# Output products two tiles behind the hidden products, in the expert stage of an attention and mixture-of-experts kernel

## The chip, the core and the metric

The kernel runs on one core of one Trainium2 chip. The metric is the device time of one execution in microseconds (us), as the median of several runs. The core's engines each work through a queue of their own, in the order in which the program was laid out: PE (TensorE, matrix products; its weight loads are listed apart as PEld), DVE (VectorE), ACT (ScalarE), POOL (GpSimd) and SP (SyncE, which here only starts transfers). Transfers (DMA) are also started from ACT and POOL. An instruction waits until the semaphores it needs are set, and everything behind it in the same queue waits with it.

## The reference, cut to what matters

Three stages follow one another. An attention between 512 tokens and 32 state rows, for 8 batches of 8 heads, gives 4352 rows of 512 numbers. A mixture of experts sends each row to one of 8 experts, 544 rows to each. A gated feed-forward layer closes.

```python
def _moe_ref(x, w_gate, w1, w2):
    ...
    for idx in order:                       # logits, from the largest down
        tok, e = (int(idx) // E, int(idx) % E)
        if assigned[tok] >= 0 or counts[e] >= cap:
            continue
        assigned[tok] = e
        counts[e] += 1
    ...
    for e in range(E):
        mask = assigned == e
        h = np.maximum(x[mask] @ w1[e], 0.0)
        out[mask] = h @ w2[e]

def _moe2_ref(x, w_gate, w_val, w_out):
    g = x @ w_gate
    silu = g * (1.0 / (1.0 + np.exp(-g)))
    return silu * (x @ w_val) @ w_out
```

w1 of an expert is 512 x 1024, w2 is 1024 x 512. The three matrices of the last layer arrive as 64-bit floats and are converted on the core.

## The kernel before

The attention takes the first 187 us of the profiled span, the experts run until about 691 us, and the last layer takes the rest. The change is in the experts.

**Tiles.** The 544 rows of an expert are worked in two halves, of 256 and 288 rows. For each half the 1024 hidden values come in 8 tiles of 128. So tile number u = 16 x expert + 8 x half + f, with f from 0 to 7, and there are 128 tiles. A matrix product of two 32-bit operands is done as three products of a high and a low part. `hidden` (L788) forms one tile of relu(x w1): 12 matmuls into the PSUM tile `h` (two buffers), then ACT writes the high part `hh` (L802) and DVE the low part `hl` (L803), each in a tile with two buffers. `expert_out` (L806) adds the tile's share of h w2 to the four PSUM tiles y0 to y3 (one buffer each): 8 matmuls that read `hh` (L813, L814) and 4 that read `hl` (L817). After f = 7 the four y tiles are copied to `ys`, y1 and y3 by ACT (L823), y0 and y2 by DVE (L825), and sent to memory. The next half's first output product writes the same four PSUM tiles, so it waits for these copies.

**Order.** The loop at the end of the stage (L995) issues, for each u, whatever the table `plan` holds for that u, then `hidden(u)`, then `expert_out(u-1)`. From there a scheduler lays out each engine's queue; `issue_after` ties an instruction behind a named one on its engine.

**What is woven in.** `plan` places between the tiles: the selection of the next expert's rows (`select`), a chain of short steps that go back and forth between DVE and PE (search steps L432 to L474, then the placement: sums over `C`, comparison `I` L421, `rh` L541, and 34 small matmuls L548 that read `rh`); the gathering of the selected rows and their transposition on PE through the PSUM tile `bt`, which has one buffer (`turn`, L777; ACT copies it to `xh` L782 and DVE to `xl` L783); the loading of the next expert's weights, 8 transfers of 512 KB, each followed by a cast on ACT (L725) and a subtraction on DVE (L726); and the conversion of the last layer's weights, in 36 pieces: `load64` starts a 512 KB transfer into `raw64` from ACT's queue (L167), and three tiles later `convert` scales it on ACT (`mag`, L175) and joins it on DVE (`f32v`, L177, L178, L180). The 36 transfers are planned at u = 10 + 3.2 n, so every fifth stands at u = 16k + 10, behind the hidden product of tile 16k + 9.

**Afterwards.** The last layer's operand tiles `yb` lie in a ring of 14 tiles of 4 KB per partition, split over two pools, `cy` and `cy2`, by `NY`.

Of the kernel before, what the change touches and what calls it, by code (L numbers as in the profile page):

```python
# [22 lines left out]
FR = mybir.dt.float32r  # L23
# [17 lines left out]
ROW = D + 1 + E  # L41
NT = 5
NW = 24
NY = (8, 6)
EARLY = 6
P_ = {'spin': 12, 'xl': 2, 'pc': (0, 9), 'ct': 12, 'cuts': (0, 34), 'lead': [0, 1, 10, 25, 44, 57, 73, 89], 'hook': ['p', 'p', 'p', 'p', 'p', 'x', 'p', 'p'], 'w': [8, 14, 8, 8, 8, 8, 8, 8], 'whook': 'h', 'g': [0, 3, 18, 36, 56, 70, 85, 103], 'gs': 0.34, 't': [0, 14, 29, 46, 61, 75, 91, 104], 'ts': 1, 'ghook': 'p', 'thook': None, 't0': (2, 4, 5), 'l0': 10, 'lp': 3.2, 'cd': 3, 'lhook': 'hh', 'chook': 'h', 'swap': [], 'y0': 16, 'f0': [10, 4, 3]}
PRE = 24
# [5 lines left out]
def f32(ap):  # L53
    return ap.bitcast(F32)
# [3 lines left out]
def moe_kernel(ctx: ExitStack, tc: tile.TileContext, x, state, moe_w_gate, moe_w1, moe_w2,  # L58
# [648 lines left out]
    bw = b_ctx.enter_context(tc.tile_pool(name="bw", bufs=2, reuse_waits="tile"))  # L707
# [81 lines left out]
    def hidden(i, hf, f):  # L789
        xh, xl = XT[i][hf]  # L790
        T = 256 + 32 * hf
        ph = bp.tile([128, 288], F32, name="h", bufs=2)[:, :T]
        fs = slice(128 * f, 128 * f + 128)
        terms = [(k, q) for k in range(4) for q in range(3)]
        if 16 * i + 8 * hf + f < P_["xl"]:
            terms.sort(key=lambda kq: kq[1])
        for n, (k, q) in enumerate(terms):
            hooks["p"] = nc.tensor.matmul(ph, W[i][0][k][q == 1][:, fs], (xl if q == 2 else xh)[:, k, :T],  # L798
                                          start=(n == 0), stop=(n == 11)).ins
        hh = bw.tile([128, 288], FR, name="hh")[:, :T]  # L800
        hl = bw.tile([128, 288], FR, name="hl")[:, :T]
        relu[16 * i + 8 * hf + f] = hooks["hh"] = nc.scalar.activation(hh, ph, AF.Relu).ins  # L802
        hooks["h"] = nc.vector.scalar_tensor_tensor(hl, ph, 0.0, f32(hh), op0=OP.max, op1=OP.subtract).ins  # L803
        return hh, hl

    def expert_out(i, hf, f, hh, hl):  # L806
        if f == 0:
            py[i, hf] = [bp.tile([128, 288], F32, name=f"y{d}")[:, :256 + 32 * hf] for d in range(4)]
        p = py[i, hf]
        wh, wl = W[i][1][f // 2]  # L810
        for d in range(4):
            ds_ = slice(128 * d, 128 * d + 128)
            nc.tensor.matmul(p[d], wh[:, f % 2, ds_], hh, start=(f == 0), stop=False)  # L813
            nc.tensor.matmul(p[d], wl[:, f % 2, ds_], hh, start=False, stop=False)  # L814
        for d in range(4):
            ds_ = slice(128 * d, 128 * d + 128)
            nc.tensor.matmul(p[d], wh[:, f % 2, ds_], hl, start=False, stop=(f == 7))  # L817
        if f == 7:
            T = 256 + 32 * hf
            ys = bw.tile([128, 4, 288], F32, name="ys", bufs=1)  # L820
            for d in range(4):
                if d % 2:
                    nc.scalar.copy(ys[:, d, :T], p[d])  # L823
                else:
                    nc.vector.tensor_copy(ys[:, d, :T], p[d])  # L825
            if hf == 0:
                nc.sync.dma_start(y_d[i][:, :, :256], ys[:, :, :256])
            else:
                nc.sync.dma_start(y_d[i][:, :, 256:], ys[:, :, :256])
                nc.sync.dma_start(yt_d[:, :, i, :], ys[:, :, 256:])  # L830
# [111 lines left out]
    def ring_tile():  # L942
        n = ring[0] % sum(NY)
        ring[0] += 1
        if n < NY[0]:
            return cy.tile([128, 2, 2, 256], FR, name="yb")
        return cy2.tile([128, 2, 2, 256], FR, name="yb")
# [44 lines left out]
        at(int(P_["l0"] + P_["lp"] * n), P_["lhook"], load64, n)  # L992
        at(int(P_["l0"] + P_["lp"] * n + P_["cd"]), P_["chook"], convert, n)

    pend = None  # L995
    for u in range(16 * E):
        i, hf, f = u // 16, u // 8 % 2, u % 8
        for hook, fn, args in plan.get(u, []):
            if hook:
                with tc.issue_after(hooks[hook]):  # L1000
                    fn(*args)
            else:
                fn(*args)
        if u in P_["swap"] and pend:
            expert_out(*pend)
            pend = None
        h = hidden(i, hf, f)
        if pend:
            expert_out(*pend)
        pend = (i, hf, f) + h  # L1010
    expert_out(*pend)
    sel_ctx.close()
    cy = ctx.enter_context(tc.tile_pool(name="cy", bufs=NY[0], side="right", reuse_waits="tile"))
    with tc.issue_after(relu[16 * E - P_["y0"]]):
# [12 lines left out]

    cy2 = ctx.enter_context(tc.tile_pool(name="cy2", bufs=NY[1], reuse_waits="tile"))
    cw = ctx.enter_context(tc.tile_pool(name="cw", bufs=1, reuse_waits="tile"))
# [281 lines left out]
```

## Time and profile before

| | us |
|---|---|
| median of 3 runs | 1485.01 |
| lowest and highest run | 1481.55, 1488.06 |
| profiled execution | 1485.12 |
| its span in the trace | 1483.5 |
| PE busy in the span | 1384.4 (93%) |
| DVE busy | 1126.4 (76%) |
| ACT busy | 571.0 (38%) |
| POOL busy | 468.2 (32%) |

The span is 1.6 us shorter than the profiled execution's own time. The profile gives, for each engine, how long it was busy, which instruction waited and what ended the wait ("releaser"), and the clock that TensorE was granted: 1.00 is its upper level of 2.4 GHz, 0.50 the lower of 1.2 GHz; a mean in between over a stretch says which part of it ran at which level. Of the chain of work that ended last, 71% is PE, 11% DVE, 8% DMA and 3% ACT.

### The profile page before, as it was taken

Reading aid. Unit: us, or ns where it says so; the run is one execution under the profiler, and the core shown is the slowest. Engines: PE = TensorE matmul, PEld = TensorE weight load, DVE = VectorE, ACT = ScalarE, POOL = GpSimd, SP = SyncE. Lnnn points to the kernel's source line nnn. Section 1 sums busy time; section 2 is a strip of 40 time slices with the busy share of each in tenths; the row PEclk is TensorE's granted clock in tenths of the full one; section 3 lists DMA queues with packets and bytes.
Section 4 is the critical chain, followed back from the end, with each engine's and each line's share of the span. In section 5 each row is a group of like instructions: output and inputs, shape, how many; then the busy total and the mean of one; then the engine's idle time right before and its main releaser. Section 6 shows DMA issues by size and latency. Waiting matters only on the chain.

```text
span 1483.5 us, 29094 instructions
## 1 busy us (share of the span) xinstructions
PE 1384.4 (93%) x11440; PEld 1335.4 (90%) x11441; DVE 1126.4 (76%) x2152; ACT 571.0 (38%) x1124; POOL 468.2 (32%) x398
## 2 busy tenths in 40 slices
PE   6998389998999999999999999999999999999997
PEld 5776278988988899999999999999999999999996
DVE  5898768876777765586888677976856797999982
ACT  5885124332332333343323232522323264444441
POOL 4775331100111001152553410012131002778872
PEclk9999579999999999999999999999999999999999
DMA  7542225545444356455665553635465378334431
GB/s 129 124 113 91 97 77 192 188 155 192 147 163 160 126 197 213 164 181 199 225 237 192 192 185 115 234 143 192 173 213 204 129 246 294 119 138 144 151 118 43
DMA packets 125417, 244.67 MB, mean 165 GB/s; under 512 B 48096, under 2 KB 57312, under 8 KB 118624
## 3 DMA queue, kind: packets, MB, share of 16 engines
q1 hardware_dynamic: 107696, 203.46, 40.6%
q10 hardware_dynamic: 11472, 19.43, 4.2%
q0 software_dynamic: 6112, 19.93, 3.9%
q8 instruction: 89, 1.46, 0.4%
q14 instruction: 48, 0.39, 0.1%
HBM read 157.84 MB, written 84.93 MB: 164 GB/s over the span
## 4 chain that ended last, share of the span: by engine, by line
PE 71%; DVE 11%; DMA 8%; issue 4%; ACT 3%; POOL 2%; SPq 0%; POOLq 0%; DVEq 0%; ACTq 0%
PE b L1044 44%; PE h L798 11%; PE y L817 4%; PE y L813 4%; PE y L814 3%; DMA raw<-in_moe_w_out_dram 2%; DMA raw<-v_d 1%; DMA raw<-in_moe_w_gate_dram 1%; DMA raw<-in_moe_w_val_dram 1%; DVE w L726 1%; PE bt L777 1%; DMA xc<-in_x_dram 1%; DVE xw L320 1%; DVE yb L842 1%; DMA raw<-in_moe_w_dram 1%
## 5 line engine op out<-in xcount | busy, mean ns | idle before, releaser
L1044 PE MATMUL b<-yb,w 128*128 128x256 f32 x4320 | 517.5, 282 | 6.9 <-DVE cs L1084 5.7
L1044 PEld LDWEIGHTS b<-yb,w 128*128 128x128 f32 x4320 | 515.0, 190 | 9.3 <-DVE cs L1084 7.2
L1044 PE MATMUL b<-w,yb 128*128 128x256 f32 x2160 | 257.2, 282 | 0.0
L1044 PEld LDWEIGHTS b<-w,yb 128*128 128x128 f32 x2160 | 257.0, 190 | 0.0
L798 PE MATMUL h<-xh,w 128*128 128x288 f32 (+1 forms) x1024 | 215.4, 303 | 0.7 <-issue 0.7
L798 PEld LDWEIGHTS h<-xh,w 128*128 128x128 f32 x1024 | 167.8, 197 | 1.7 <-issue 1.1
L768 POOL DMA_INDIRECT xg<-xm_d,idx x38 | 48.1, 1265 | 367.8 <-PE bt L777 163.4
L842 DVE TENSOR_TENSOR yb<-tt,yb 128x512 fp32r<-128x512 f32 x164 | 143.7, 893 | 14.4 <-ACT yb L841 14.4
L813 PE MATMUL y<-hh,w 128*128 128x288 f32 (+1 forms) x512 | 140.2, 300 | 12.6 <-DVE ys L825 4.8
L798 PE MATMUL h<-xl,w 128*128 128x288 f32 (+1 forms) x512 | 151.9, 299 | 0.0
L841 ACT CAST yb<-tt 128x512 fp32r<-128x512 f32 x164 | 101.2, 620 | 104.6 <-PE b L1044 87.8
L814 PE MATMUL y<-hh,w 128*128 128x288 f32 (+1 forms) x512 | 139.2, 298 | 0.0
L842 DVE TENSOR_TENSOR yb<-raw,yb 128x512 fp32r<-128x512 f32 x127 | 126.0, 1000 | 15.8 <-ACT yb L841 13.5
L864 POOL TENSOR_TENSOR tt<-raw 128x512 f32<-128x512 f32 (+1 forms) x33 | 42.0, 1277 | 286.9 <-DMA raw<-m_d 212.9
L802 ACT ACTIVATE hh<-h 128x288 fp32r<-128x288 f32 (+1 forms) x128 | 50.7, 397 | 199.2 <-PE h L798 177.5
L813 PEld LDWEIGHTS y<-hh,w 128*128 128x128 f32 x512 | 98.7, 194 | 14.9 <-ACT ys L823 6.3
L803 DVE SCALAR_TENSOR_TENSOR hl<-h,hh 128x288 fp32r<-128x288 f32 (+1 forms) x128 | 55.5, 435 | 69.6 <-ACT hh L802 63.7
L841 ACT CAST yb<-raw 128x512 fp32r<-128x512 f32 x127 | 78.1, 620 | 63.5 <-PE b L1044 50.2
L798 PEld LDWEIGHTS h<-xl,w 128*128 128x128 f32 x512 | 99.5, 196 | 0.2
L814 PEld LDWEIGHTS y<-hh,w 128*128 128x128 f32 x512 | 98.7, 194 | 0.3
L817 PE MATMUL y<-hl,w 128*128 128x288 f32 (+1 forms) x512 | 94.9, 300 | 2.2 <-DVE hl L803 2.2
L726 DVE TENSOR_TENSOR w<-raw,w 128x1024 fp32r<-128x1024 f32 x61 | 73.8, 1238 | 16.1 <-ACT w L725 15.4
(253 smaller groups left out, 2107.7 us busy)
## 6 DMA issues: line engine op xcount, KB each, us to landing
raw<-in_moe_w_dram SPq DMA_DIRECT2D x60, 512.0 KB
raw<-m_d SPq DMA_DIRECT2D x30, 1024.0 KB
m_d<-m SPq DMA_DIRECT2D x48, 512.0 KB
raw<-v_d SPq DMA_DIRECT2D x32, 512.0 KB
raw<-y_d SPq DMA_DIRECT2D x14, 1024.0 KB
v_d<-f32v SPq DMA_DIRECT2D x36, 256.0 KB
xm_d<-xm SPq DMA_DIRECT2D x8, 1024.0 KB
y_d<-ys SPq DMA_DIRECT2D x16, 512.0 KB
```

What stands on the lines that cost most here:

```text
L726: eng.tensor_tensor(lo, raw, f32(hi), OP.subtract)
L768: hooks["g"] = nc.gpsimd.indirect_dma_start(out=xg[:n], out_offset=None, in_=xm_d, in_offset=bass.IndirectOffsetOnAxis(ap=idx[i][:n, j:j + ...
L798: hooks["p"] = nc.tensor.matmul(ph, W[i][0][k][q == 1][:, fs], (xl if q == 2 else xh)[:, k, :T], start=(n == 0), stop=(n == 11)).ins
L802: relu[16 * i + 8 * hf + f] = hooks["hh"] = nc.scalar.activation(hh, ph, AF.Relu).ins
L803: hooks["h"] = nc.vector.scalar_tensor_tensor(hl, ph, 0.0, f32(hh), op0=OP.max, op1=OP.subtract).ins
L813: nc.tensor.matmul(p[d], wh[:, f % 2, ds_], hh, start=(f == 0), stop=False)
L814: nc.tensor.matmul(p[d], wl[:, f % 2, ds_], hh, start=False, stop=False)
L817: nc.tensor.matmul(p[d], wh[:, f % 2, ds_], hl, start=False, stop=(f == 7))
L841: nc.scalar.copy(hi, src)
L842: nc.vector.tensor_tensor(lo, src, f32(hi), OP.subtract)
L864: nc.gpsimd.tensor_tensor(S1, a21, a22, OP.add)
L1044: nc.tensor.matmul(p[:, q], a(x, q), b(y), skip_group_check=True, start=start and not (q or n or m), stop=stop and q == 1 and n == last an ...
```

## The change

The output products no longer follow one tile behind but two. `pend` becomes a list: after each `hidden` the oldest entries are worked off until two are left, or one where f = 0. So in a half the order is hidden(u), expert_out(u-2), except at its ends: behind hidden of f = 0 the last two output products of the half before come one after the other, and behind hidden of f = 1 there is none. `hh` and `hl` get a third buffer (2 x 288 x 4 = 2304 bytes more per partition), and the ring's split becomes 7 and 7 tiles. The branch on `swap`, an empty list, goes.

```diff
-NY = (8, 6)
+NY = (7, 7)
...
-        hh = bw.tile([128, 288], FR, name="hh")[:, :T]
-        hl = bw.tile([128, 288], FR, name="hl")[:, :T]
+        hh = bw.tile([128, 288], FR, name="hh", bufs=3)[:, :T]
+        hl = bw.tile([128, 288], FR, name="hl", bufs=3)[:, :T]
...
-    pend = None
+    pend = []
     for u in range(16 * E):
         i, hf, f = u // 16, u // 8 % 2, u % 8
...
-        if u in P_["swap"] and pend:
-            expert_out(*pend)
-            pend = None
-        h = hidden(i, hf, f)
-        if pend:
-            expert_out(*pend)
-        pend = (i, hf, f) + h
-    expert_out(*pend)
+        pend.append((i, hf, f) + hidden(i, hf, f))
+        while len(pend) > (1 if f == 0 else 2):
+            expert_out(*pend.pop(0))
+    for p in pend:
+        expert_out(*p)
```

The scheduler's order moves with it. First, PE at the border between tiles 111 and 112 (expert 6 to 7): from the last output matmul of the old half to the first of the new. `h_8677` is the hidden product of tile 113, `h_8694` below that of tile 114. Before:

```order
5228 L817 MATMUL y3_8412<-hl_8617,w_7611 128x288
5229 L798 MATMUL h_8677<-xh_8236,w_8286 128x256
...
5240 L798 MATMUL h_8677<-xl_8237,w_8304 128x256
5241 L813 MATMUL y0_8694<-hh_8654,w_8310 128x256
5242 L814 MATMUL y0_8694<-hh_8654,w_8311 128x256
```

And with the change:

```order
5236 L817 MATMUL y3_8438<-hl_8605,w_7599 128x288
5237 L798 MATMUL h_8677<-xh_8224,w_8274 128x256
...
5248 L798 MATMUL h_8677<-xl_8225,w_8292 128x256
5249 L798 MATMUL h_8694<-xh_8224,w_8274 128x256
...
5260 L798 MATMUL h_8694<-xl_8225,w_8292 128x256
5261 L813 MATMUL y0_8711<-hh_8642,w_8298 128x256
```

Two hidden products of 12 matmuls stand between the old half's last output matmul and the new half's first, where one stood. At the borders to tiles 32 and 64 the scheduler sets the first half of the new output product (y1 and y3), and the 34 placement matmuls behind it, between the two hidden products.

Second, ACT around the conversion that is loaded behind tile 105 (expert 6), where `hh_8405` is tile 105's. Before:

```order
523 L802 ACTIVATE hh_8405<-h_8392 128x288
524 L167 DMA raw64_8432<-in_moe2_w_gate_dram 128x2x512
525 L782 CAST xh_8238<-bt_8425 128x4x128
526 L175 ACTIVATE mag_8536<-raw64_8432 128x512
527 L802 ACTIVATE hh_8447<-h_8434 128x288
528 L725 CAST w_8310<-raw_8308 128x1024
529 L782 CAST xh_8238<-bt_8463 128x4x128
```

And with the change:

```order
523 L802 ACTIVATE hh_8405<-h_8392 128x288
524 L167 DMA raw64_8416<-in_moe2_w_gate_dram 128x2x512
525 L782 CAST xh_8226<-bt_8409 128x4x128
526 L802 ACTIVATE hh_8431<-h_8418 128x288
527 L175 ACTIVATE mag_8524<-raw64_8416 128x512
528 L782 CAST xh_8226<-bt_8451 128x4x128
529 L802 ACTIVATE hh_8471<-h_8458 128x288
```

The `hh` of tile 106 now stands ahead of `mag`, which waits for the transfer, instead of behind it; the copy of the next turned tile (`xh_8226<-bt_8451`) stands behind `mag`. Over all 36 pieces, 27 had one `hh` between the start of the transfer and `mag` and 9 had none; now 32 have one and 4 none.

Third, DVE at the placement of the last expert's rows, around tiles 89 and 90. Before:

```order
1098 L421 TENSOR_TENSOR I_7693<-IE_172,lo_7681 128x4352
1099 L726 TENSOR_TENSOR w_7594<-raw_7591,w_7593 128x1024
1100 L541 TENSOR_TENSOR rh_7690<-T6_7688,rq_1588 128x34x6 x2
1101 L803 SCALAR_TENSOR_TENSOR hl_7790<-h_7776,hh_7789 128x288
1102 L783 TENSOR_TENSOR xl_7449<-bt_7805,xh_7448 128x4x128
```

And with the change:

```order
1089 L421 TENSOR_TENSOR I_7693<-IE_172,lo_7681 128x4352
1090 L541 TENSOR_TENSOR rh_7690<-T6_7688,rq_1588 128x34x6 x2
1091 L803 SCALAR_TENSOR_TENSOR hl_7774<-h_7760,hh_7773 128x288
1092 L783 TENSOR_TENSOR xl_7437<-bt_7793,xh_7436 128x4x128
1093 L552 COPY dp_7730<-acc_7694 128x12
```

`rh` no longer stands behind the weight subtraction `w`. In the last layer the order of PE, ACT and DVE is the same as before.

## Rows read from the trace of the kernel before

**Rows 1.** Busy time by stretch: engines' us (instructions), granted clock, DMA share, GB/s.

```profile
187.00:691.00 504.00, 473.46 (x4120) 450.96 (x4120) 366.74 (x916) 171.77 (x328) 81.59 (x71) 0.96 0.49 165
```

**Rows 2.** Waits of PE, 187 to 700 us: total us, times, longest.

```profile
PE y L813 <- DVE ys L825: 4.8, 3, 2.0
PE y L813 <- ACT ys L823: 4.0, 2, 2.5
PE y L813 <- ACT hh L802: 3.9, 2, 2.4
PE y L817 <- DVE hl L803: 2.2, 3, 1.4
```

**Rows 3.** Timeline of PE where it idled: start, duration, instruction, idle time before.

```profile
342.12 0.39 PE L813 MATMUL y<-hh,w 128*128 128x256 f32 x1 [1.52 <-ACT hh L802]
368.21 1.05 PE L432 MATMUL acc<-G,I 128*128 128x8 bf16 x34 [2.53 <-DVE need L581]
422.15 0.40 PE L813 MATMUL y<-hh,w 128*128 128x288 f32 x1 [1.03 <-DVE ys L825]
430.76 0.16 PE L470 MATMUL acc<-fe,unit 32*128 32x8 bf16 x1 [2.24 <-DVE fe L468]
460.87 0.58 PE L813 MATMUL y<-hh,w 128*128 128x256 f32 x1 [2.55 <-ACT ys L823]
496.76 0.16 PE L470 MATMUL acc<-fe,unit 32*128 32x8 bf16 x1 [2.51 <-DVE fe L468]
527.25 0.39 PE L813 MATMUL y<-hh,w 128*128 128x256 f32 x1 [1.40 <-ACT ys L823]
564.25 1.01 PE L548 MATMUL acc<-rh,I 128*128 128x12 bf16 x34 [3.10 <-DVE rh L541]
620.65 0.47 PE L813 MATMUL y<-hh,w 128*128 128x288 f32 x1 [2.37 <-ACT hh L802]
643.43 0.36 PE L813 MATMUL y<-hh,w 128*128 128x256 f32 x1 [1.72 <-DVE ys L825]
668.93 0.38 PE L813 MATMUL y<-hh,w 128*128 128x288 f32 x1 [2.05 <-DVE ys L825]
```

**Rows 4.** Timeline of ACT and its DMA queue (ACTq): three conversion loads.

```profile
451.18 0.35 ACTq L167 DMA_DIRECT2D raw<-in_moe_w_out_dram  x1
459.87 0.66 ACT L175 ACTIVATE mag<-raw 128x512 f32<-128x512 f32 x1 [4.68 <-DMA raw<-in_moe_w_out_dram]
...
553.59 0.39 ACTq L167 DMA_DIRECT2D raw<-in_moe_w_gate_dram  x1
560.78 0.66 ACT L175 ACTIVATE mag<-raw 128x512 f32<-128x512 f32 x1 [3.60 <-DMA raw<-in_moe_w_gate_dram]
...
611.07 0.41 ACTq L167 DMA_DIRECT2D raw<-in_moe_w_gate_dram  x1
619.64 0.66 ACT L175 ACTIVATE mag<-raw 128x512 f32<-128x512 f32 x1 [5.94 <-DMA raw<-in_moe_w_gate_dram]
```

**Rows 5.** Stretches of 8 us behind three of the stalls; clock third from the end.

```profile
430.00:438.00 8.00, 7.24 (x68) 6.34 (x67) 5.25 (x15) 1.92 (x4) 0.00 (x0) 1.00 0.03 11
460.00:468.00 8.00, 7.13 (x65) 7.04 (x66) 3.12 (x16) 1.96 (x6) 2.55 (x3) 0.57 0.43 136
496.00:504.00 8.00, 7.24 (x52) 6.47 (x51) 5.25 (x13) 2.28 (x5) 0.95 (x1) 0.79 0.13 37
```

**Rows 6.** Chain of waits: one product of 12 matmuls, 256 and 288 wide.

```profile
281.00 1.43 PE h L798 x12
...
670.76 1.59 PE h L798 x12
```

**Rows 7.** Timeline of DVE, before the placement matmuls and before tile 120's product.

```profile
562.40 1.22 DVE L726 TENSOR_TENSOR w<-raw,w 128x1024 fp32r<-128x1024 f32 x1 [3.39 <-ACT w L725]
563.55 0.64 DVE L541 TENSOR_TENSOR rh<-T,rq 128x204 bf16<-128x204 bf16 x2
...
669.04 0.68 DVE L178 SCALAR_TENSOR_TENSOR f32v<-mag,f32v 128x512 int32<-128x512 int32 x1
```

## The prediction

> **What bounds the kernel now.** I read the busy time by stretch first. In the expert stretch PE works 473.46 of 504.00 us and DVE 366.74, at a mean granted clock of 0.96 [rows 1]. So PE sets the time there, and two things are to be had: about 30 us in which it idles, and the time at the lower clock. The change touches nothing that the attention or the last layer computes, so the sum is made over this stretch.
>
> Next come PE's waits, grouped by what ended them [rows 2]. The output products waited 8.8 us for the copies `ys` that free the four y tiles (4.8 for DVE, 4.0 for ACT), 3.9 us for `hh` and 2.2 us for `hl`: 14.9 us, half of the idle time. These are the waits that a longer lag can reach. The rest is mostly selection, small matmuls that wait for DVE.
>
> PE's timeline shows where the large ones lie [rows 3]: five waits for `ys` (1.03, 2.55, 1.40, 1.72, 2.05 us; all at the first output product of a new half), two for `hh` (1.52, 2.37), and four of the selection (2.53, 2.24, 2.51, 3.10).
>
> Then the queue that is late. ACT starts a conversion load and some instructions later stands at `mag` until it lands: 8.7 us after the start in the first pair of rows, 7.2 and 8.6 in the others, with ACT idle for 3.60 to 5.94 us [rows 4]. All that is queued behind `mag` is late with it: `hh`, the `ys` copies, weight casts, and through them DVE. The loads behind tile 16k+9 meet the next expert's weights, and there the four selection waits and the `hh` wait of 2.37 us lie.
>
> Last, the clock. After the wait of 2.55 us the next 8 us ran at 0.57, after 2.51 us at 0.79; after 2.24 us at 1.00 [rows 5]. What that costs is 8 x (1 - clock): 3.4 and 1.7 us. The stretch behind 368.21 read 0.57 as well, and those behind 527.25, 564.25 and 620.65 read 0.79; behind 342.12, 422.15, 643.43 and 668.93 the clock stayed up. So these six falls cost 2 x 3.4 + 4 x 1.7 = 13.6 us. Which stall brings a fall is not a matter of its length alone, since 1.40 us did and 2.05 us did not.
>
> **The change part by part.** A product of 12 matmuls takes 1.43 us at 256 columns and 1.59 us at 288 [rows 6]; I call that a phase. No matmul is added or removed; the number of phases is the same, and only their order differs.
>
> *At a border of halves* the new half's first output product waits for the old half's copies. Between them stood one hidden product, now two [the order of PE in the section on the change]: 1.43 to 1.59 us more cover. Counted from work tied to the old half's last tile, an output product comes in as well, so 2.9 to 3.2 us. By place:
> - 422.15 (tile 56): 1.03 goes to 0.
> - 460.87 (tile 64): `ys` stands behind `mag` in both orders, and here the first half of the output product stays ahead of the second hidden product, so only one phase comes in: 2.55 - 1.6 = 0.95.
> - 527.25 (tile 80): 1.40 goes, but the 34 placement matmuls now stand inside the hidden product of tile 81 and wait for `rh`. The trace of before has no such wait here; it lies between 0 and the 3.10 of 564.25. I take 0.9, what 564.25 comes to below.
> - 643.43 (tile 112): 1.72 against 3.0 more: 0. Three more ACT casts now precede `ys`, so up to 1.72 may stay.
> - 668.93 (tile 120): 2.05 - 3.0, but two conversion steps of 0.68 [rows 7] now precede the copies on DVE: 0.4.
> Together 8.75 to 2.25: 6.5 us gained. If DVE's backlog is as late as its worst row, the gain falls to 4.
>
> *Waits for `hh`.* At 342.12 `mag` stood ahead of the next `hh`; now it stands behind it, and the output product comes two phases later: 1.52 goes. The placement matmuls come two tiles earlier there, and I take 0.8 for them (0 to 3.10, as above). Gain 0.7. At 620.65 the order of ACT changes likewise, but one `xh` copy now stands behind `mag`. PE's fifth transposition needs the single `bt` tile, hence that copy and the subtraction on DVE. From tile 105's `hh` PE has two transpositions, two hidden and two output products to do, about 7.3 us; `mag` ends at 619.64 + 0.66 - 611.07 = 9.2, and two steps near 0.68 [rows 7] follow: 10.5. A wait of 3.2 in place of 2.37: 0.8 lost, bounded by 1.6 either way (one phase).
>
> *Behind tile 16k+9* the lag works backwards. No output product follows f = 1, so from there to any later hidden product, and to the selection steps tied to it, PE has one phase less to do, while the load takes as long as before. Four selection waits lie there:
> - 368.21: 1.6 less cover, but `need` now goes ahead of the weight subtraction (1.22 [rows 7]): 0.4 more.
> - 430.76 and 496.76: the step that meets `mag`'s delay is a later one; I take 0.3 and 0.9 more (at 496.76 a turned tile's subtraction goes ahead of it). Bounds are 0 and 1.6 each.
> - 564.25: `rh` stood behind a weight subtraction (562.40 to 563.62) that had waited 3.39 us for its cast; DVE had been free since 559.01 [rows 7]. Now `rh` goes first and could end at 559.01 + 0.64 = 559.7. PE arrived at 564.25 - 3.10 = 561.15, now 2.4 earlier by the order (the placement stands in tile 91, not in tile 90's output product): 558.8. Wait 0.9, gain 2.2; not below 0, so the gain is 3.10 at most.
> Net 0.6 gained.
>
> *Early tiles.* Of the 2.2 us for `hl` [rows 2], 0.6 and a placement wait beside it go and a wait for tile 9's `hl` comes; I take 0.4 gained. The wait of 1.4 in the first tiles stays, since the next search step waits for the same DVE chain.
>
> *Buffers and pools.* The third `hh` and `hl` buffers cost no instruction. The ring's eighth tile moves to the pool that opens after the experts; its first write comes about 15 us later, with seven tiles ready. I take 0; the wait that the last layer already has at 715 us could move by as much as 3 us either way.
>
> Direct: 6.5 + 0.7 - 0.8 + 0.6 + 0.4 = 7.4 us. Clock: with 460.87, 527.25 and 564.25 below 1.1 us, I take their falls as gone (3.4 + 1.7 + 1.7), since 1.03 brought none; a longer wait near 430.76 may bring one (1.7). Net 5.1. The bounds are 0 (new falls elsewhere) and 10. Sum: 12.5 us off the profiled 1485.12, about **1473 us**; the median of the runs, 1485.01, is the same number.
>
> The Trainium skill has a rule against this: in "TensorE: Matmul & The Clock Gate", section "HAM oscillation", a kernel whose matmuls waited for transfers was helped by the order of its loop, and PSUM double-buffering on top gave no further gain. By it the time would stay near 1485, the first rival's side; the waits at 368.21 to 496.76 agree with it, and the five for `ys`, of which three lie behind no load, do not.
>
> **The rivals.**
> *The waits only move (no change).* Half of the stalls come from loads that land when they land. If the five places behind tile 16k+9 (368.21, 430.76, 496.76, 564.25, 620.65) each lose a whole phase, 5 x 1.6 = 8 in place of the net 0.2 lost above, and the clock falls as often as now, 6.5 + 0.7 + 0.4 - 8 = -0.4: 1485.5; with the clock's gain at 460.87 and 527.25 kept, 1480. For it: those loads take 7.2 to 8.6 us [rows 4] against four or five phases of PE's work. Against: 564.25 and 368.21 lose a subtraction ahead of them.
>
> *The border costs more than it gives (slower).* Behind f = 1, hidden(8k+3) needs the `h` tile that hidden(8k+1) wrote, so `hl` of 8k+1 has 3.2 us where it had 4.2, and the single `bt` tile is asked for a phase earlier. If at the six loads behind 16k+9 from 295 us on PE loses 1.6 us and the clock falls to 0.57 each time (6 x 3.4 = 20.4 in place of the 8.5 now at 368, 496, 564 and 620): +9.6 + 11.9 - 7.6 (`ys`, `hh`, early) - 5.1 (clock at 460, 527) = +8.8: 1494. It decides once each of the six costs over 3.4 us more than now. For it: the falls follow just such stalls. Against: `hh` of 8k+2 now stands ahead of `mag`.
>
> *All of it goes.* If the selection finds DVE free as well, 14.9 of `ys`, `hh` and `hl` and 10 of clock: 1460. Against: that chain alternates PE and DVE whatever the lag.
>
> That the change doesn't do what it says is excluded by PE's order, but for tiles 32 and 64.
>
> **How the numbers follow.** Forecast (1467 to 1478) 0.54; waits only move (1479 to 1489) 0.28; slower 0.10; all goes 0.08. The range takes the forecast and most of the first rival: 1465 to 1488. A measurement of this kernel can tell about 0.5%, or 7.4 us, from no change. Faster by more: 0.50 of the forecast and the 0.08, 0.57 together; slower by more: 0.10; same: 0.33.
>
> **What would show it.** Right: PE's waits for `ys` fall from 8.8 us below 3 and those for `hh` and `hl` below 2; no fall of the clock behind tiles 64 and 80; the wait for `rh` near tile 91 below 1.5 us; a wait of PE's transposition for `xl` near tile 108. Wrong: waits of L798 for `hl` or `hh` (the `h` tile not free) of more than 3 us in total, falls of the clock at places that had none, or idle time of PE in the experts that is not below 26 us.

## The result, and the profile after

The change makes the kernel faster: 1469.4 us against 1481.4 (medians of 8 runs each), ratio 0.9919, 95% interval 0.9895 to 0.9943. In a later session (6 runs, 11 of before) it was 1473.3 against 1483.2, ratio 0.9936 (0.9911 to 0.9961). The forecast was 1473, which is 12.5 us less than the profiled 1485.1; the medians lie 12.0 apart.

The gain lies where the sum was made. The first view is busy time by stretch, from the first hidden product of tile 0 to the end of tile 127's output product; the columns are the stretch, its length, PE's busy time, its matmuls, the mean granted clock, the DMA share and GB/s. Before:

```profile
188.30:691.48 503.18, 473.31 (x4121) 0.96 0.49 165
```

After, in its first profile:

```profile
188.44:679.06 490.62, 467.71 (x4121) 0.96 0.51 169
```

And in a second profile of the same kernel:

```profile
185.46:675.42 489.96, 467.26 (x4120) 0.96 0.50 169
```

The stretch is 12.6 and 13.2 us shorter. The matmuls are the same, so length minus busy is idle time, and a change of busy time is put down to the clock. Idle time fell from 29.9 to 22.9 and 22.7 us, busy time by 5.6 and 6.1. The forecast was 7.4 of waits and 5.1 of clock. In the first profile the whole span fell by only 9.2, from 1483.5 to 1474.3, because there the last layer took 795.2 us for 792.0. In the second profile it took 791.5. So the order alone does not bring that loss, which stays an open point below; the first profiled execution was also the slowest of its eight, at 1475.9.

PE's waits in the experts after the change (engine, line and tile, what ended the wait: total us, times, longest), for the groups of [rows 2]:

```profile
PE bt L777 <- DMA xg<-xm_d,idx: 3.9, 1, 3.9
PE bt L777 <- DVE xl L783: 3.2, 2, 1.9
PE acc L432 <- DVE G L406: 3.1, 1, 3.1
PE h L798 <- DVE hl L803: 2.5, 3, 1.4
PE acc L466 <- DVE ev L463: 2.5, 3, 2.0
PE y L813 <- DVE ys L825: 2.0, 3, 0.9
...
PE y L813 <- ACT ys L823: 0.6, 2, 0.3
```

The waits for `ys` went from 8.8 to 2.6 us (1.4 of it at the five places of [rows 3], the rest at two borders that had none), those of the output products for `hh` from 3.9 to none. Three of the large groups are new: the transposition that waits for gathered rows, the one that waits for `xl`, and the search step that waits for `G`. The first and the last lie together in time, as PE's timeline shows (start, duration, instruction; in brackets the idle time before it and what ended it). These rows answer to [rows 3]:

```profile
247.71 0.66 PE L777 MATMUL bt<-ident,xg 128*128 128x128 f32 x4 [3.87 <-DMA xg<-xm_d,idx]
...
251.52 1.17 PE L432 MATMUL acc<-G,I 128*128 128x8 bf16 x34 [3.14 <-DVE G L406]
...
371.52 1.03 PE L432 MATMUL acc<-G,I 128*128 128x8 bf16 x34 [1.99 <-DVE need L581]
...
494.51 0.24 PE L466 MATMUL acc<-ev,SL 128*32 128x8 f16 x4 [1.98 <-DVE ev L463]
...
555.87 0.66 PE L777 MATMUL bt<-ident,xg 128*128 128x128 f32 x4 [1.25 <-DVE xl L783]
...
610.08 0.43 PE L777 MATMUL bt<-ident,xg 32*128 32x32 f32 x4 [1.93 <-DVE xl L783]
...
658.14 0.37 PE L813 MATMUL y<-hh,w 128*128 128x288 f32 x1 [0.88 <-DVE ys L825]
```

At the first two rows PE stands for 7 us of 8. Nothing like it was there before: in the same stretch of before PE was busy all the time, though the DMA was as full.

```profile
238.00:246.00 8.00, 7.89 (x60) 1.00 1.01 369
246.00:254.00 8.00, 8.00 (x96) 1.00 0.39 116
```

After:

```profile
238.00:246.00 8.00, 5.06 (x34) 1.00 0.97 320
246.00:254.00 8.00, 3.12 (x44) 0.68 0.37 131
```

The gather starts on POOL at 239.61 and its rows are there at 247.7. Before, it started at 237.73, and the transposition stood two products later in PE's queue, so nothing was seen of it.

Last, the clock in stretches of 8 us, as in [rows 5]:

```profile
250.00:258.00 8.00, 6.46 (x72) 0.64 0.22 43
372.00:380.00 8.00, 8.00 (x65) 0.58 0.24 68
434.00:442.00 8.00, 7.78 (x67) 1.00 0.31 99
460.00:468.00 8.00, 7.71 (x91) 1.00 0.74 236
494.00:502.00 8.00, 7.49 (x54) 0.79 0.04 12
527.00:535.00 8.00, 8.00 (x70) 1.00 0.68 213
555.00:563.00 8.00, 7.13 (x55) 1.00 0.53 171
610.00:618.00 8.00, 7.92 (x49) 0.79 0.52 163
```

The falls behind tiles 64, 80 and 91 are gone, none came near 430, those at 372, 494 and 610 stayed, and one is new at 250.

### The profile page after: what moved, and what is told of

It reads as the page before. It is cut to its first block, busy times and chain, and to the rows that moved or that the text cites. A ratio compares the mean times of both kernels' runs of the same rounds, so it can differ in the third digit from the quotient of the medians.

```text
span 1474.3 us, 29106 instructions
## 1 busy us (share of the span) xinstructions
PE 1381.2 (94%) x11441; PEld 1334.0 (90%) x11441; DVE 1121.4 (76%) x2152; ACT 570.2 (39%) x1124; POOL 465.5 (32%) x398
## 4 chain that ended last, share of the span: by engine, by line
PE 72%; DVE 10%; DMA 8%; issue 5%; ACT 3%; POOL 1%; SPq 0%; POOLq 0%; DVEq 0%; ACTq 0%
PE b L1041 48%; PE h L798 10%; PE y L813 3%; PE y L817 3%; PE y L814 3%; DMA raw<-in_moe_w_val_dram 1%; DMA raw<-in_moe_w_gate_dram 1%; DMA raw<-in_moe_w_out_dram 1%; PE bt L777 1%; DMA raw<-v_d 1%; DMA xg<-xm_d,idx 1%; DVE xw L320 1%; DMA raw<-in_moe_w_dram 1%; DVE xTl L232 1%; DVE I L421 1%
## 5 line engine op out<-in xcount | busy, mean ns | idle before, releaser
L813 PE MATMUL y<-hh,w 128*128 128x288 f32 (+1 forms) x512 | 137.6, 295 | 2.6 <-DVE ys L825 2.0
L814 PE MATMUL y<-hh,w 128*128 128x288 f32 (+1 forms) x512 | 136.7, 293 | 0.0
L817 PE MATMUL y<-hl,w 128*128 128x288 f32 (+1 forms) x512 | 91.0, 295 | 0.0
L1048 ACT ACTIVATE m<-b 128x256 f32<-128x256 f32 x60 | 22.9, 383 | 165.0 <-PE b L1041 147.7
```

The source lines that it names most:

```text
L1048: nc.scalar.activation(m, g, AF.Sigmoid)
```

## The experiments

The theory held that the lag covers the copies `ys` and ACT's standing at `mag`, and that the new wait near 248 us limits the gain. The rivals: one of the parts (border, lag inside a half, buffers) does all of it, or the lag only covers the loads. In the table, the stretch and PE's idle time in it are from one profile each (first hidden product to last output product, as above).

| kernel | stretch | idle | median | ratio to before, 95% |
|---|---|---|---|---|
| before | 503.2 | 29.9 | 1481.4 | |
| changed | 490.6 | 22.9 | 1469.4 | 0.9919 (0.9895 to 0.9943) |
| changed, again | 490.0 | 22.7 | 1473.3 | 0.9936 (0.9911 to 0.9961) |
| border only | 497.9 | 27.6 | 1477.9 | 0.9981 (0.9960 to 1.0002) |
| inside a half only | 491.1 | 25.2 | 1474.9 | 0.9980 (0.9960 to 1.0001) |
| buffers only | 503.7 | 29.1 | 1477.4 | 0.9993 (0.9969 to 1.0017) |
| two buffers | 486.0 | 21.9 | 1471.2 | 0.9948 (0.9926 to 0.9970) |
| before, convert later | 490.7 | 22.5 | 1471.8 | 0.9932 (0.9905 to 0.9958) |
| changed, turn later | 491.5 | 22.5 | 1472.0 | 0.9913 (0.9883 to 0.9942) |
| changed, convert later | 488.4 | 22.5 | 1465.2 | 0.9896 (0.9870 to 0.9922) |
| both (turn and convert later) | 480.2 | 19.5 | 1462.7 | 0.9871 (0.9845 to 0.9897) |
| both, selection later | 480.2 | 16.2 | 1458.0 | 0.9859 (0.9829 to 0.9888) |
| changed, lag of three | 487.3 | 22.2 | 1470.0 | 0.9948 (0.9927 to 0.9969) |

Medians of before differ between sessions: 1480.0 beside the four kernels from "border only" to "two buffers", 1483.2 beside "changed, again", "before, convert later", "changed, turn later" and "both", and 1478.9 beside the last three that were made ("changed, convert later", "both, selection later", the lag of three). So kernels of different sessions are compared by their ratios.

The columns "stretch" and "idle" are of one execution each, and two things in them are no effect of an edit. The profiled executions of the changed kernel (the first), "border only", "changed, convert later" and "both, selection later" were the slowest of their kernels, 6.5 to 9.3 us above the median. And the clock of the first 30 us of the stretch differed: it read 0.73 or 0.74 in eight profiles, those of before and both of the changed kernel among them, but 0.81 in "border only" and "both, selection later", 0.84 in "inside a half only", and 0.89 in "two buffers" and in "both". The hidden product of tile 8 starts 38.5 us into the stretch in the changed kernel and in "changed, convert later", 34.1 us into it in "both", though these three have the same order up to there. So 4.4 us of what "both" seems to gain in its stretch belong to that execution.

**Border only.**

```diff
-        while len(pend) > (1 if f == 0 else 2):
+        while len(pend) > (2 if f == 1 else 1):
```

> Only the border of two halves is changed: two hidden products stand between the old half's last output product and the new half's first, and inside a half the output product follows one tile behind, as before. Theory (the gain lies at the border): PE's waits for ys fall from 8.8 us to under 3, the falls of the clock behind tiles 64 and 80 go, the waits of the output products for hh (3.9 us) stay, and PE has no wait for the gathered rows near 248 us; 1468 to 1474 us, ratio to before 0.991 to 0.996. Rival (the gain is the lag inside a half): 1478 to 1483, ratio over 0.997.

Measured: 1477.9, ratio 0.9981. `ys` fell to 1.8 us, as the theory said, and there was no wait for gathered rows. But the 1.8 us lie at tile 80, where the fall of the clock stayed (0.79 in 520 to 528), and the stretch gained only 5.3. PE's waits show where the rest went:

```profile
PE acc L466 <- DVE ev L463: 4.0, 2, 2.1
...
PE bt L777 <- DVE xl L783: 3.6, 1, 3.6
...
PE y L813 <- ACT ys L823: 1.8, 1, 1.8
PE y L813 <- ACT hh L802: 1.7, 1, 1.7
```

The selection's waits for `ev` were 1.0 before and are 4.0, while those for `fe` went from 5.9 to 1.5; in all the selection waits as long as before (15.7 us for 14.9). The wait for `xl` is new. Taking the `ys` waits away brings PE sooner to the next late thing. The theory that the gain lies at the border falls.

**Lag inside a half only.**

```diff
-        while len(pend) > (1 if f == 0 else 2):
+        while len(pend) > (1 if f < 2 else 2):
```

> The counterpart: the output products follow two tiles behind inside a half, but at a border only one hidden product stands between the halves, as before. Theory (border): PE's waits for ys stay at 6 us or more, those for hh go, the wait for the gathered rows near 248 us is there as in the changed kernel; 1476 to 1484 us, ratio 0.996 to 1.002. Rival (lag inside a half): 1468 to 1474, ratio under 0.995, with the hh waits gone.

Measured: 1474.9, ratio 0.9980, a time between the two ranges. By the ratio neither part alone can be told from no change, though the median of this one lies 5.1 us below that of before in the session and the border's 2.1. In its profile the stretch is 12.1 us shorter. Some 3 of that were gained before tile 8, which starts 3.1 us sooner than in the changed kernel; the rest is still more than the border's 5.3. The expectation for `ys` failed:

```profile
PE y L813 <- DVE ys L825: 2.5, 1, 2.5
...
PE y L813 <- ACT yb L841: 1.7, 1, 1.7
```

Only 4.2 us are left of 8.8, though one hidden product stands at the border as before. (The 1.7 are the wait at the border to tile 112; the view puts them down to `yb`, which stands behind the copies `ys` in ACT's queue.) So either phase alone covers over half of the `ys` waits, which is why the two parts do not add there. A likely reason, argued and not shown: with a second output product behind the new half's first hidden product, `hh` and `hl` of the new tile are done before the old half's y tiles are complete, and no longer hold up the copies.

**Buffers only.** The order of before, with the third `hh` and `hl` and the ring's split:

```diff
-NY = (8, 6)
+NY = (7, 7)
...
+        hh = bw.tile([128, 288], FR, name="hh", bufs=3)[:, :T]
+        hl = bw.tile([128, 288], FR, name="hl", bufs=3)[:, :T]
```

> The order of before with only the third hh and hl buffers and the ring's tiles divided 7 and 7. Theory: nothing, 1478 to 1484, ratio 0.998 to 1.002, the waits for ys and hh as before. Rival (the buffers or the pools carry the gain): 1467 to 1474, ratio under 0.995.

Measured: 1477.4, ratio 0.9993, the waits as before (`ys` 9.4, `hh` 4.0). The buffers alone do nothing that can be told from no change, as forecast.

**Two buffers.** The new order with those lines as before.

> The new order with two hh and hl buffers and the ring divided 8 and 6, as before. Theory (the order carries the gain; a relu that waits for the output product before it is one phase late and has a phase of room): 1468 to 1477, ratio 0.991 to 0.997. Rival (the third buffer is needed, since relu and the hl subtraction hold up all that is queued behind them on ACT and DVE): 1481 or more, with waits of the hidden products for hl over 5 us.

Measured: 1471.2, ratio 0.9948. The hidden products' waits for `hl` were 3.0 us, not over 5. The order carries the gain; that the third buffer adds to it is not shown, since the intervals overlap.

**The changed kernel again.**

> The changed kernel once more, on the chip of the three runs beside it and with a second profile. Theory (its first profile, at 1475.9 us, stands above its own median by 6.5 us, and the loss lies in attention and the last layer): 1467 to 1473 us, ratio to before 0.990 to 0.996; again a wait of 2 to 5 us of PE's transposition for the gathered rows near 248 us, one of about 3 us for the next selection step, and a clock below 0.7 behind them. Rival (that wait was an accident of one execution): no wait over 1 us there.

Measured: 1473.3, ratio 0.9936, just above the expected 1467 to 1473. The waits near 245 us were there again, 3.14 for the rows and 3.14 for `G`. They belong to the order, not to one execution.

**Transposition later.**

```diff
-            at(P_["t"][k] + int(j * P_["ts"]), P_["thook"], turn, k, j)
+            at(P_["t"][k] + int(j * P_["ts"]), "p" if k == 1 and j == 0 else None, turn, k, j)
```

> The changed kernel, but the first transposition of expert 1 is tied to the hidden product of tile 13, so that it stands behind the output product of tile 11 in PE's queue instead of in front of the selection for expert 2. Theory (that transposition waits for its gather and holds up the selection behind it, 3.9 + 3.1 us and a fall of the clock of 3 us): the waits at 247 to 255 us fall from 7 to under 2 us, the clock stays over 0.9 there, and 1459 to 1466 us, ratio to before 0.985 to 0.991, 0.994 to 0.997 of the changed kernel. Rival (the selection only waits for something else, or the later transpositions delay the first tiles of expert 1): within 2 us of the changed kernel.

Measured: 1472.0, beside 1473.3 for the changed kernel on the same chip: the rival. The wait for rows is gone, but PE's timeline shows what took its place:

```profile
241.63 0.18 PE L580 MATMUL acc<-crb,onesb 128*128 128x8 bf16 x1 [1.29 <-DVE crb L578]
...
244.95 1.17 PE L432 MATMUL acc<-G,I 128*128 128x8 bf16 x34 [3.14 <-DVE G L406]
```

The 3.14 us stayed to the hundredth, and so did the fall of the clock (0.57 in 242 to 250). In this kernel's order, as in the changed one's, the 34 matmuls of L432 stand right behind the one of L580, with no product of the experts between. DVE's rows of the changed kernel show what they wait for:

```profile
248.44 0.17 DVE L581 TENSOR_SCALAR need<-acc 128x8 f32<-128x8 f32 x1 [3.02 <-PE acc L580]
...
251.03 0.43 DVE L406 TENSOR_TENSOR G<-w,am 128x272 bf16<-128x272 f32 x1
```

DVE stands at `need` until L580 is done, and `G` is six instructions behind it, 3.0 us. `G` itself takes nothing from `need` or from L580; it is late because its steps stand behind `need` in DVE's queue. That wait of 3.14 is in all seven profiles whose queue has L580 and L432 side by side here, and in none of the six where a product stands between (before, border only, buffers only, two buffers, before with the conversion later, and the selection later). My theory blamed the transposition for this wait; it is the selection's order.

**Conversion later, on the order of before.** Each of the 36 weight conversions follows its load by four tiles, not three:

```diff
-P_ = {... 'cd': 3, ...}
+P_ = {... 'cd': 4, ...}
```

> The order of before, but each weight conversion follows its load by four tiles instead of three, so that ACT does not stand at mag until the load lands. Theory (half of what the lag gains is cover for ACT standing at mag, the rest is the border itself): the waits for hh (3.9 us) and the ys wait of tile 64 go, ys keeps 4 to 6 us at the other borders, the clock falls at 460, 497, 564 or 620 become fewer; 1471 to 1478 us, ratio 0.994 to 0.999. Rival (all of the gain is cover for ACT at mag): ys under 2 us as well, 1464 to 1471, ratio under 0.993.

Measured: 1471.8, ratio 0.9932, a little more gain than the theory expected: as much as the change's, by another way. ACT's waits at `mag` for the load, in the experts, before:

```profile
ACT mag L175 <- DMA raw<-in_moe_w_val_dram: 21.6, 7, 8.0
ACT mag L175 <- DMA raw<-in_moe_w_out_dram: 18.4, 9, 4.7
ACT mag L175 <- DMA raw<-in_moe_w_gate_dram: 14.4, 6, 5.9
...
ACT mag L175 <- DVE f32v L178: 4.2, 5, 1.7
```

With the conversion later:

```profile
ACT mag L175 <- DVE f32v L178: 33.8, 15, 4.9
...
ACT mag L175 <- DMA raw<-in_moe_w_val_dram: 14.3, 3, 6.9
ACT mag L175 <- DMA raw<-in_moe_w_gate_dram: 13.6, 3, 6.0
...
ACT mag L175 <- DMA raw<-in_moe_w_out_dram: 2.1, 1, 2.1
```

The waits for the load went from 54.4 us in 22 to 30.0 in 7. But `mag` has one buffer, so it now waits for the DVE step L178 that reads the piece before: whatever ended the wait, ACT stood at `mag` for 66.9 us before and for 71.0 with the conversion later. So the edit does not shorten ACT's standing; it changes what ACT stands for, and where. Which of this brings the gain is not shown. And of the 30.0 us, 25.5 are the five loads behind tile 16k+9, the worst ones, which took 28.4 before. In the changed kernel the waits for the load sum to 57.6 in 23 (48.4 in 20 in its second profile): the lag takes little or nothing off them, it lets PE get past them. The `ys` waits kept 4.3 us, as the theory said; that of tile 64 is gone, and the clock fell three times where it had fallen six times. The `hh` waits did not go (3.1).

**Conversion later, on the changed kernel.**

> The changed kernel with only the weight conversions four tiles behind their loads. Theory (the lag and the later conversion add, since the lag gives cover at the ends of halves and the later conversion takes ACT's standing at mag away): 1462 to 1468 us, ratio to before 0.986 to 0.992, and the wait of PE's transposition for xl near 610 us (1.9 to 2.4) under 1. Rival (the combined kernel's gain came from both edits together, and the lag covers the loads already): 1469 to 1474 us.

Measured: 1465.2, ratio 0.9896, as the theory said; but the wait for `xl` near 609 us was 2.8, where under 1 was expected. On ACT one sees why: there a single `hh` stands between the start of the load and `mag`, as in the changed kernel, and `mag` waits for the load as before, with the copy `xh` behind it.

```profile
599.09 0.39 ACTq L167 DMA_DIRECT2D raw<-in_moe_w_gate_dram  x1
...
601.01 0.41 ACT L802 ACTIVATE hh<-h 128x288 fp32r<-128x288 f32 x1 [0.90 <-PE h L798]
607.08 0.66 ACT L175 ACTIVATE mag<-raw 128x512 f32<-128x512 f32 x1 [5.65 <-DMA raw<-in_moe_w_gate_dram]
607.64 0.57 ACT L782 CAST xh<-bt 128x512 fp32r<-128x512 f32 x1
```

**Both edits together.** The two diffs above, on the changed kernel.

> The changed kernel with both edits: the first transposition of expert 1 later, and each weight conversion four tiles behind its load. Theory (the two losses that are left, near 250 us and behind tile 16k+9, are separate and add): 1454 to 1463 us, ratio to before 0.981 to 0.989, with PE's idle time in the experts under 15 us and at most two falls of the clock behind 230 us there. Rival (with two tiles of lag the loads are covered already, so the later conversion adds nothing): as the run with the later transposition alone, within 2 us.

Measured: 1462.7, ratio 0.9871, whose interval lies below that of the changed kernel in the same session. Idle time was 19.5, not under 15, the wait for `G` was still there, and the clock fell three times (near 241, 364 and 600), not at most twice.

**Selection later.** The combined kernel, and:

```diff
-P_ = {... 'hook': ['p', 'p', 'p', 'p', ...], ...}
+P_ = {... 'hook': ['p', 'p', 'h', 'p', ...], ...}
```

> The combined kernel, and the selection for expert 2 is tied to the subtraction hl of tile 10 instead of its hidden product, so that PE has a hidden product and part of an output product between the first small matmul of its new search step and the 34 that wait for DVE. Theory (it is this order, not the transposition, that brings the waits of 2.4 and 3.1 us near 240 us and the clock of 0.57 behind them): both waits under 1 us, no fall of the clock there, 1454 to 1460 us, ratio to before 0.981 to 0.986. Rival (the selection of expert 2 then ends later, and the gathers for expert 2 or a later step wait instead): 1461 to 1466 us.

Measured: 1458.0, ratio 0.9859. The 3.14 us are gone, as they must be if the order of the selection brings them. But two smaller waits stand there now, not under 1 us as expected:

```profile
244.42 0.18 PE L580 MATMUL acc<-crb,onesb 128*128 128x8 bf16 x1 [1.75 <-DVE crb L578]
...
245.93 0.85 PE L798 MATMUL h<-xh,w 128*128 128x288 f32 x2 [1.33 <-DVE hl L803]
```

The clock fell behind them as it did in the combined kernel (0.57 in 245 to 253; there 0.57 in 241 to 249), where no fall was expected. Idle time fell by 3.3 us, and yet the stretch is as long as the combined kernel's. The difference lies in the first 30 us, where both have the same order. Combined, and with the selection later:

```profile
187.11:217.11 30.00, 27.07 (x247) 0.89 0.21 73
...
189.23:219.23 30.00, 25.12 (x211) 0.81 0.21 74
```

The profiled execution was the slowest of this kernel, 9.3 us above its median. The two ratios overlap, so the times do not show that this edit adds to the combined kernel. It has the lowest ratio of the study; its interval lies below the changed kernel's.

**A lag of three.** Four `hh` and `hl` buffers, and:

```diff
-        while len(pend) > (1 if f == 0 else 2):
+        while len(pend) > min(3, f + 1):
```

> The changed kernel with output products three tiles behind, and four hh and hl buffers. Theory (two tiles already cover ys and hh, of which under 3 us of waits are left, and what remains is selection, which the lag does not reach): 1467 to 1476 us, ratio to before 0.990 to 0.998, ys waits under 3 us as with two. Rival (more of the same cover still helps): under 1466 us, ratio under 0.990.

Measured: 1470.0, ratio 0.9948, as the theory said. No wait for `ys` is left, and another came:

```profile
PE h L798 <- DVE hl L803: 6.2, 3, 4.7
```

The longest of them, 4.74 at 625.47, is at tile 115, where on DVE steps of the last layer's operands (`yb`) stand ahead of `hl`.

## Why the prediction was right, point by point

The time was right, 1473 for 1469.4 and 1473.3, and so were the two sums: 7.0 and 7.2 us of idle time for 7.4 forecast, 5.6 and 6.1 of busy time for 5.1 of clock. The mechanism, more cover for the waits on `ys` and `hh`, was right too. But inside the first sum errors cancelled, and that it came so near is in part luck: all steps but the early tiles were to give 7.0 us and gave about 14, and the early tiles, which were to give 0.4, lost about 7 (13 and 6 in the second profile).

- *Border.* 8.75 to 2.25 was forecast; 1.4 at these places (2.6 with two other borders) and 1.3 were measured. That both phases count, as the step had it, is shown by the two halves of the change, which leave 1.8 and 4.2.
- *`hh` at 342.12.* Gone. The 0.8 set against it for `rh` did not come.
- *620.65.* The mechanism was right: PE's transposition waits for `xl` behind `mag`. The size was 1.93 and 2.37, not 3.2, because that load took 7.2 us, not the 8.6 of [rows 4].
- *Behind tile 16k+9.* The four selection waits, 10.4 us in [rows 3], were forecast to give 0.6 and came to 5.5 (1.99, 0.23, 1.98, 1.25) and 6.2 in the second profile. So this step was mis-sized by about 4, to the good. The loads there were quicker than in the kernel before [rows 4]; at tile 41, `mag` begins 7.3 us after the load's start:

```profile
362.68 0.35 ACTq L167 DMA_DIRECT2D raw<-in_moe_w_out_dram  x1
...
369.95 0.66 ACT L175 ACTIVATE mag<-raw 128x512 f32<-128x512 f32 x1 [5.26 <-DMA raw<-in_moe_w_out_dram]
```

  Over the five places the loads took 6.9 us on average after the change (7.2 in the second profile) for 7.9 before. Why they are quicker was not tried, nor whether that is all of the 4 us. Near tile 91 `rh` no longer waits, but the transposition does, 1.25 for `xl`.
- *Early tiles.* This is the step that failed. It counted 0.4 us gained and took in only `hl` and the placement. The new order also moves the first transposition of expert 1 forward, and with it the 34 matmuls of L432 next to L580: 7.0 us (6.3 in the second profile) and a fall of the clock that cost 8 x 0.36 = 2.9. The order of PE showed both, and the trace of before showed a gather that starts at 237.73, 10 us ahead of its transposition; the two were not compared at this place.
- *Clock.* Of the falls at 460, 527 and 564 all three went, as forecast (6.8 us). The one feared near 430 did not come, but one at 250 did (2.9). That is 3.9 net; the busy time fell by 5.6 and 6.1, and the rest was not traced.
- *Buffers and pools.* 0, shown by the buffers alone.

The Trainium skill, "TensorE: Matmul & The Clock Gate", section "HAM oscillation", was cited for no further gain from more buffering. With buffers alone no gain was measured here either (0.9993), though `hh` and `hl` are not the PSUM tiles of which it speaks. It does not speak against a change of order, by which the time did fall; as a reason for a time near 1485 it was misplaced.

The first rival (waits only move) holds for parts of the change: the border alone moved most of what it took away. The slower rival did not come near its point: no load behind 16k+9 cost PE more than 2.4 us. Of the signs that were named, those for right came (but for the waits on `hl`: 2.5 us at the hidden products, where under 2 was named), and so did one of those for wrong, a fall of the clock at a place that had none (250). The shares 0.50 and 0.08 that were added for "faster by more" make 0.58, not 0.57.

One thing stays open. Five profiles, the changed kernel's first among them, spend 3 to 8 us more in the last layer than before (1483.5 - 691.48 = 792.0). In all five PE waits 3.0 to 5.8 us there for ACT's copy `s`, where before it waited 0.5, and ACT stands 7.0 to 8.7 us for one weight piece, where in the other eight it stands 4.1 to 6.5. In the changed kernel:

```profile
865.96 0.62 ACT L841 CAST w<-raw 128x512 fp32r<-128x512 f32 x1 [7.07 <-DMA raw<-v_d]
```

The second profile of the same kernel has 4.41 there and no such wait of PE, so the order alone does not decide it. Nor is the piece all of it: of PE's two waits for `s` in the changed kernel, 1.70 lies behind this row and 2.04 ahead of it; and before with the conversion later has 3.4 us of such waits at a loss of only 1.3. What decides it was not found.

## What to carry to other kernels

A longer lag between producer and consumer does not make a late queue earlier; it lets PE pass it, and one phase often did here, so a third tile of lag gave nothing more. Moving the instruction that the late queue stands at (starting a conversion one tile later) gave as much, and the two together gave more; but ACT stood there as long as before, so count the waits of such an instruction for every releaser and not for one alone. When an order is changed, look in the new queue for every instruction that moved next to one on whose result it hangs, be it only through the queue of another engine, and even far from the place the change is meant for. And before two profiles are compared, compare a stretch that no edit reaches.

## What the runs showed that was not expected

- Where the 34 matmuls of a search step stand right behind the small one for which DVE stands at `need`, PE waits 3.14 us, equal to the hundredth in seven profiles: the time of DVE's chain alone.
- With the conversion a tile later, ACT's waits at `mag` for the load fell from 54.4 to 30.0 us, and those for DVE's `f32v` rose from 4.2 to 33.8.
- The clock of the first 30 us of the experts read from 0.73 to 0.89 in kernels with the same order there ("changed, convert later" and "both").
- A gather behind a full DMA (share 0.97 in 238 to 246) took 8.1 us from its start on POOL to the transposition that used its rows.
- What the clock does is not a matter of one wait's length: 1.99 us at 371 brought 0.58, 1.93 at 610 brought 0.79, and 2.24 at 430 in the kernel before left 1.00 [rows 3, 5].
